# Attention products in 64-row and 64-column parts, two chunks in a bank for block 0, and an order by due times

## The chip, the cores and the metric

The kernel runs on one core of a Trainium2 chip. The metric is the device time of one execution in microseconds; before the change its median over three runs is 845.69 (844.81 to 847.82). In the text TensorE, VectorE, ScalarE, GpSimd and SyncE stand for the engines that the profile calls PE, DVE, ACT, POOL and SP.

## What is computed

A linear attention (4 batches, 8 heads, 576 tokens, 64 columns a head) gives 2304 tokens of 512 columns. Two feed-forward layers follow: a gated one of width 1536 behind a norm over the token, and an elu one of width 2048. All in fp32.

```
kv  = einsum('bhsd,bhse->bhde', k, v)
out = einsum('bhsd,bhde->bhse', q, kv)
x   = out / sqrt(mean(out * out, -1) + 1e-6) * g_norm      # per head
x   = (per token: heads side by side, 2304 x 512)
xn  = x / sqrt(mean(x * x, -1) + 1e-6) * rms_g
x   = (silu(xn @ w_gate) * (xn @ w_val)) @ w_out           # 512 -> 1536 -> 512
g   = elu(x @ w_in)                                        # 512 -> 2048
y   = g @ w_out2                                           # 2048 -> 512
```

## The kernel before

**Tiles.** The 2304 tokens are 18 tiles of 128 rows, two to a pair. Five blocks carry them through the layers: block 0 has one pair (256 columns), blocks 1 to 4 have two pairs each (512 columns), and blocks (1,2) and (3,4) also work together. A batch is 576 tokens, four and a half tiles, so tiles 4 and 13 lie across two batches. The hidden width is cut into chunks f of 128: 12 in the gated layer (phase 0), 16 in the elu layer (phase 1).

**Numbers in two parts.** Each operand of the large products is a high part (h_g, xh, act 0) and a low part (l_g, xl, act 1), and a product is three of them: high by high, low by high, high by low. A weight comes from memory as raw (raw_g) and is taken apart by `conversion` (line 401): c_g, w_g, then h_g on ScalarE and l_g on VectorE. For names in the list `SPARE` two of its steps run on ScalarE (lines 412 and 435) and not on VectorE (lines 414 and 437).

**Attention.** `sum_kv` (line 260) adds the k by v products of one tile into the bank of its batch: four products of two heads each, 128 by 128, of which only the two 64 by 64 blocks on the diagonal are wanted. `keep_kv` copies these blocks into a buffer whose other blocks were set to zero. `attend` (line 295) multiplies q of one tile with that buffer, four products of 128 by 128 into one bank po; a tile across two batches does it for each half of its tokens, with 64 columns of weights. On po follow the square on ScalarE (line 313), the mean on VectorE (317), the power on GpSimd (324), the product with it on VectorE (327), the product with g_norm (333), the same over the whole token (338 to 345), and `turn` (line 353), which transposes a pair into banks pt. From pt, line 371 makes xh (ScalarE) and line 369 xl (VectorE). An fp32 product is two matmul instructions in the trace.

**The layers.** hid_g and hid_v (line 754) are the products of the first weights for one f and one block, named hid_g(phase, f, block). The pair units pu and pb (lines 552 and 920) do two f, two blocks at a time. The way back b(group, block, chunk) (line 654) multiplies with w_out; for all but the last group its bank is copied by ScalarE (line 692) and added to `mid` in memory by a transfer of GpSimd's queue (line 698); the first group is written by SyncE. For the last group the sum so far is fetched (line 717) and added on VectorE (line 728, far), and xh and xl of the next layer come from that (lines 1305 and 1308), with sums T of blocks for the pair units (976 to 983).

**The order.** Nothing is written in the program's order by hand. Every piece of work is a step of `Plan` with an engine, a length, the steps it needs and the banks or buffers it takes. `run` (line 73) goes through time: on each engine it takes the ready step that can start first, and among those within 0.03 us the one with the lowest rank, a number written by hand (100 + 100 i for tile i's attention, higher for later f). The buffers are given out in the same pass. The order that results is the program of each engine.

## Time and profile before

| | us |
|---|---|
| median of three runs | 845.69 |
| profiled execution | 845.66 |
| span of the profiled execution | 843.9 |
| TensorE busy | 830.4 (98%) |
| VectorE busy | 742.2 (88%) |
| ScalarE busy | 593.0 (70%) |
| GpSimd busy | 228.5 (27%) |

Phase 0 begins within the attention at about 38 us, the pair units at about 100, and phase 1 at about 470. Busy time of TensorE is that of matmuls whose ends overlap, so a full stretch shows no idle time, and what a piece of work costs is read from start to start: a group of n alike instructions lasts n - 1 of these steps and one instruction's own time (0.27 us for a small fp32 matmul). A line of a stretch gives busy time, the granted clock as a share of 2.4 GHz, and how much of the 16 DMA engines' time was used.

### The profile page before, as it was taken

How to read it: one execution, taken by the hardware profiler on the slowest of the kernel's cores; microseconds unless marked ns; L12 is line 12 of the kernel's file. 1: busy time of each engine (PE TensorE's matmuls, PEld its weight loads, DVE VectorE, ACT ScalarE, POOL GpSimd, SP SyncE). 2: the span in 40 equal slices, each digit the busy share in tenths (PEclk: the TensorE clock that was granted, in tenths of full speed). 3: DMA queues.
4: the chain of work that ended last, by engine and by line, in shares of the span. 5: the costliest groups of instructions: out<-in, count | busy, mean ns of one | idle time of the engine just before them, and what ended most of it. 6: DMA issues, size and time to landing. Idle time of an engine off the chain costs nothing.

```text
span 843.9 us, 12231 instructions
## 1 busy us (share of the span) xinstructions
PE 830.4 (98%) x4108; PEld 695.2 (82%) x4108; DVE 742.2 (88%) x1375; ACT 593.0 (70%) x1149; POOL 228.5 (27%) x260
## 2 busy tenths in 40 slices
...
PEclk9999999999999999999999999999999999999999
...
GB/s 361 365 161 44 124 159 180 109 163 166 46 55 148 149 75 136 125 65 134 142 187 94 81 141 154 144 150 125 162 189 137 116 150 207 105 146 156 159 264 208
DMA packets 57375, 126.14 MB, mean 149 GB/s; under 512 B 6496, under 2 KB 10080, under 8 KB 57312
## 3 DMA queue, kind: packets, MB, share of 16 engines
...
HBM read 59.28 MB, written 66.06 MB: 149 GB/s over the span
## 4 chain that ended last, share of the span: by engine, by line
PE 82%; DVE 10%; DMA 3%; ACT 2%; issue 1%; SPq 0%; ACTq 0%; DVEq 0%
PE b L654 15%; PE hid_v L754 4%; PE hid_g L754 4%; PE po L304 2%; PE hid_i L754 2%; DMA wacc<-in_q 1%; DVE far L728 1%; PE kv L268 1%; DMA wacc<-in_kv 1%; DVE T L983 1%; DVE act L608 1%; DVE xl L1308 1%; DVE far L976 1%; PE pt L359 1%; PE ('pu', 1, 0, 3)_a L552 1%
## 5 line engine op out<-in xcount | busy, mean ns | idle before, releaser
L952 POOL DMA_DIRECT2D out<-part x80 | 70.3, 965 | 259.6 <-DVE part L939 211.0
L952 POOL DMA_DIRECT2D mid<-part x48 | 42.5, 970 | 149.0 <-DVE part L939 128.3
L654 PE MATMUL b<-act,h_o 128*128 128x512 f32 (+1 forms) x288 | 78.4, 358 | 1.3 <-DVE far L728 0.7
L698 POOL DMA_DIRECT2D mid<-part x52 | 46.6, 989 | 92.8 <-ACT part L692 89.3
L692 ACT ACTIVATE part<-b 128x512 f32<-128x512 f32 (+1 forms) x118 | 62.9, 552 | 9.8 <-PE b L654 5.0
L654 PEld LDWEIGHTS b<-act,h_o 128*128 128x128 f32 x288 | 51.0, 188 | 12.3 <-DVE far L728 1.8
L654 PE MATMUL b<-act,h_p 128*128 128x512 f32 x192 | 59.8, 392 | 1.4 <-ACT part L692 0.7
L654 PE MATMUL b<-act,l_o 128*128 128x512 f32 (+1 forms) x144 | 51.0, 354 | 0.0
L795 ACT ACTIVATE e<-e 128x512 f32<-128x512 f32 (+1 forms) x80 | 46.5, 590 | 0.7
L654 PEld LDWEIGHTS b<-act,h_p 128*128 128x128 f32 x192 | 35.7, 188 | 9.8 <-ACT part L692 1.3
L654 PE MATMUL b<-act,l_p 128*128 128x512 f32 x96 | 37.4, 389 | 0.0
L324 POOL TENSOR_TENSOR ri<-ms,nhalf 128x8 f32<-128x8 f32 x18 | 31.3, 1759 | 13.9 <-DVE ms L320 13.9
L754 PE MATMUL hid_g<-xh,h_g 128*128 128x256 f32 (+1 forms) x96 | 32.9, 343 | 0.0
L754 PE MATMUL hid_g<-xl,h_g 128*128 128x256 f32 (+1 forms) x96 | 32.5, 338 | 0.3 <-DVE xl L369 0.3
L698 POOL DMA_DIRECT2D out<-part x28 | 24.6, 895 | 30.0 <-ACT part L692 29.6
L754 PE MATMUL hid_v<-xh,h_v 128*128 128x256 f32 (+1 forms) x96 | 32.5, 339 | 0.0
L754 PE MATMUL hid_g<-xh,l_g 128*128 128x256 f32 (+1 forms) x96 | 32.3, 337 | 0.0
L754 PE MATMUL hid_v<-xh,l_v 128*128 128x256 f32 (+1 forms) x96 | 32.3, 336 | 0.0
L754 PE MATMUL hid_v<-xl,h_v 128*128 128x256 f32 (+1 forms) x96 | 32.3, 336 | 0.0
L728 DVE TENSOR_TENSOR far<-far,b 128x512 f32<-128x512 f32 (+1 forms) x38 | 24.2, 654 | 8.9 <-PE b L654 5.9
L654 PEld LDWEIGHTS b<-act,l_o 128*128 128x128 f32 x144 | 27.1, 188 | 3.8
L885 DVE TENSOR_TENSOR e<-e,e 128x512 f32<-128x512 f32 x40 | 27.3, 684 | 0.0
...
## 6 DMA issues: line engine op xcount, KB each, us to landing
out<-part POOLq DMA_DIRECT2D x108, 256.0 KB, 6.1
...
```

What stands on the lines that cost most here:

```text
L268: nc.tensor.matmul(kv_acc[b][:, p, :], in_sb[i][r0:r1, p * P:(p + 1) * P], in_sb[i][r0:r1, DM + p * P:DM + (p + 1) * P], start=(i == tiles ...
L304: nc.tensor.matmul(po[r:r1, p * P:(p + 1) * P], qt[:, p, r:r1], kv_sb[b][:, p, :], start=True, stop=True)
L324: nc.gpsimd.tensor_tensor(ri, ms_t.pop(i), nhalf, op=ALU.pow)
L359: nc.tensor.transpose(pt[:, c, k * P:(k + 1) * P], x, ident)
L654: nc.tensor.matmul(po, l, r, start=f == fs[0] and i == 0, stop=f == fs[-1] and i == 2)
L692: nc.scalar.activation(x, pbank["b", k, t, e][:, :n], AF.Copy)
L698: nc.gpsimd.dma_start(out=where(ph, t, e), in_=live.pop(key), accum_op=ALU.add)
L728: nc.vector.tensor_tensor(x, x, pbank["b", k, t, e][:, :n], op=ALU.add)
L754: nc.tensor.matmul(pbank[key], l, r, start=c == 0 and i == 0, stop=c == KD - 1 and i == 2)
L795: nc.scalar.activation(live[key], live[key], AF.Exp, scale=-1.0)
L885: nc.vector.tensor_tensor(raw(*into), raw(*x), raw(*y), op=ALU.subtract)
L952: lambda key=key, t=t, e=e: nc.gpsimd.dma_start(out=where(ph, t, e), in_=live.pop(key), accum_op=ALU.add),
```

## The change

**Attention's products.** kv is made of eight products of a tile, one for each head: 128 rows, 64 columns of weights, 64 moving columns. Even heads go to the left half of TensorE's columns, odd ones to the right. One ScalarE copy of 128 by 256 takes the place of two, and no buffer has to be zeroed. q's products go by pairs of tiles: each has 64 rows (one head), 128 tokens of weights, 64 moving columns. Even heads fill the bank po(pair, 0), odd ones po(pair, 1). Square, mean, power and the product with it then go by pair and side, with as many instructions of the same number of elements as before; the rest goes by tile as before. A whole pair is one step of the plan.

**Block 0's way back in phase 0.** Two chunks of 256 columns share a bank, so copies, transfers, sums and low parts come as two of 512 columns in place of four of 256.

**Conversions.** `SPARE` begins at f = 2, not 4: for g, v and o of f = 2 and 3, twelve steps go from VectorE to ScalarE. The last pair unit of phase 0 takes its buffers from the attention's.

**The order.** The old pass comes first. Then up to six times: going back from TensorE's order, each step gets the latest time at which it has to be done, with the buffers as they were given out; these times become the ranks, and a second kind of pass makes a new order with the buffers fixed. The order with the earliest planned end is used.

```diff
-    def run(self):
-        waits = {n: sum(1 for _ in s["after"]) for n, s in self.steps.items()}
-        then = {}
-        for n, s in self.steps.items():
-            for x in s["after"]:
-                assert x in self.steps, (n, x)
-                then.setdefault(x, []).append(n)
+    def order(self):
+        self.holder, self.where = dict(self.held), {}
+        self.ends, self.log, self.rooms = {}, [], []
+        self.clock = dict(self.start)
...
+                if slot in self.holder:
+                    self.rooms.append((self.holder[slot], n))
...
+    def again(self):
+        after = {n: list(s["after"]) for n, s in self.steps.items()}
+        for key, taker in self.rooms:
+            after[taker] += self.users[key]
...
+    def latest(self):
+        need = {n: list(self.then.get(n, ())) for n in self.steps}
+        for key, taker in self.rooms:
+            for u in self.users[key]:
+                need[u].append(taker)
+        late, t = {}, 0.0
+        for _, n, e, length in self.log:
+            if e == "PE":
+                late[n] = t
+                t += length
+        for _, n, e, length in reversed(self.log):
+            s = self.steps[n]
+            ends = [late[x] - self.LAG[e][self.steps[x]["engine"] != e] - s["lat"] for x in need[n] if x in late]
+            here = min(ends, default=t) - length
+            late.setdefault(n, here)
+        return late
+
+    PASSES = 6
...
+        end = self.order()
+        assert end, "no step can start"
+        best = end, self.log
+        for _ in range(self.PASSES):
+            late = self.latest()
+            for n, s in self.steps.items():
+                s["rank"] = late[n]
+            end = self.again()
+            if end < best[0]:
+                best = end, self.log
+        self.log = best[1]
...
-SPARE = [f"{x}{f}" for f in range(4, 12) for x in "gvo"] + [f"{x}{f}" for f in range(2, 16) for x in "ip"]
+SEEDS = ()
+SPARE = [f"{x}{f}" for f in range(2, 12) for x in "gvo"] + [f"{x}{f}" for f in range(2, 16) for x in "ip"]
...
-        "A": AD, "A1": ["y0", "t3"], "P": P3 + K2, "U": US, "C": CS,
+        "A": AD, "A1": ["y0", "t3"], "P": P3 + K2, "U": US, "UZ": Z4 + ["t2"], "C": CS,
...
+    zz = [res.tile([P, 2, DM + 1], F32, tag=f"zz{j}", name=f"zz{j}") for j in range(Z // 2)]
+    z_sb = [zz[j // 2][:, j % 2, :] for j in range(Z)]
...
-        for p in range(KD):
-
+        for h in range(H):
+            s = slice(h % 2 * D, (h % 2 + 1) * D)
             nc.tensor.matmul(
-                kv_acc[b][:, p, :],
-                in_sb[i][r0:r1, p * P:(p + 1) * P],
-                in_sb[i][r0:r1, DM + p * P:DM + (p + 1) * P],
-                start=(i == tiles[0] and p == 0),
+                kv_acc[b][s, h // 2 * D:(h // 2 + 1) * D],
+                in_sb[i][r0:r1, h * D:(h + 1) * D],
+                in_sb[i][r0:r1, DM + h * D:DM + (h + 1) * D],
+                start=(i == tiles[0] and h < 2),
...
-    def keep_kv(b, h):
-        t = kv_sb[b] = kv_blocks[b % 2]
-        s = slice(h * D, (h + 1) * D)
-        nc.scalar.activation(t[s, :, s], kv_acc[b][s, :, s], AF.Copy)
+    def keep_kv(b):
+        kv_sb[b] = kv_blocks[b % 2]
+        nc.scalar.activation(kv_sb[b], kv_acc[b], AF.Copy)
...
-    def attend(i):
-
-        qt = q_sb[i // 2].rearrange("d (j a t) -> d j a t", j=2, a=KD)[:, i % 2]
-        po = bank(("po", i))
-        r = 0
-        while r < P:
-            b = (i * P + r) // seq
-            r1 = min(P, (b + 1) * seq - i * P)
-            for p in range(KD):
-                nc.tensor.matmul(
-                    po[r:r1, p * P:(p + 1) * P], qt[:, p, r:r1], kv_sb[b][:, p, :], start=True, stop=True
-                )
-            r = r1
-        po_t[i] = po.rearrange("p (h d) -> p h d", h=H)
-
-
-    def square(i):
+    def side(p, s):
+        j = 2 * p % Z
+        return zz[j // 2][:, :, :DM].rearrange("p t (a s d) -> p t a s d", s=2, d=D)[:, :, :, s]
+
+    def attend(p):
+
+        qt = q_sb[p].rearrange("d (j a t) -> d j a t", j=2, a=KD)
+        po = [bank(("po", p, s)).rearrange("p (t a d) -> p t a d", t=2, d=D) for s in range(2)]
+        for j in range(2):
+            i = 2 * p + j
+            for a in range(KD):
+                r = 0
+                while r < P:
+                    b = (i * P + r) // seq
+                    r1 = min(P, (b + 1) * seq - i * P)
+                    for s in range(2):
+                        k = slice(s * D, (s + 1) * D)
+                        nc.tensor.matmul(
+                            po[s][r:r1, j, a, :], qt[k, j, a, r:r1], kv_sb[b][k, a * D:(a + 1) * D], start=True, stop=True
+                        )
+                    r = r1
+        for s in range(2):
+            po_t[p, s] = po[s]
+
+    def square(p, s):
...
+        nc.scalar.activation(side(p, s), po_t[p, s], AF.Square, scale=D**-0.5)
+
+    def mean(p, s):
+        ms = ms_t[p, s] = sp.tile([P, H], F32, tag="ms", name=f"ms{p}_{s}")
+        nc.vector.tensor_reduce(ms.rearrange("p (t a) -> p t a", t=2), side(p, s), axis=AX.X, op=ALU.add)
+
+    def guard(p, s):
+        nc.vector.tensor_scalar(ms_t[p, s], ms_t[p, s], EPS, None, op0=ALU.add)
+
+    def invert(p, s):
+        ri = ri_t[p, s] = sp.tile([P, H], F32, tag="ri", name=f"ri{p}_{s}")
+        nc.gpsimd.tensor_tensor(ri, ms_t.pop((p, s)), nhalf, op=ALU.pow)
+
+    def norm(p, s):
+        ri = ri_t.pop((p, s)).rearrange("p (t a) -> p t a", t=2).unsqueeze(3).to_broadcast([P, 2, KD, D])
+        nc.vector.tensor_tensor(side(p, s), po_t.pop((p, s)), ri, op=ALU.mult)
...
+    KV, PO = 0.6, 1.1
...
+        if ph == 0 and t == 0:
+            for j in range(2):
+                s = slice((2 * e + j) * P, (2 * e + j + 1) * P)
+                for i, (l, r) in enumerate(((wh, ah), (wh, al), (wl, ah))):
+                    nc.tensor.matmul(
+                        po[:, j * n:(j + 1) * n], l[:, s], r, start=first and i == j == 0, stop=f == fs[-1] and i == 2,
+                        skip_group_check=True,
+                    )
+            return
...
-            return mid[:, e, a * P:(a + m) * P]
+            return mid[:, e, a * P:(a + m) * P] if t else mid[:, 2 * e:2 * e + 2, a * P:(a + m) * P]
...
-                    nc.gpsimd.dma_start(out=where(ph, t, e), in_=live.pop(key), accum_op=ALU.add)
+                    nc.gpsimd.dma_start(out=where(ph, t, e), in_=flat(live.pop(key), t or ph), accum_op=ALU.add)
...
-                nc.sync.dma_start(out=x, in_=where(ph, t, e))
+                nc.sync.dma_start(out=flat(x, t or ph), in_=where(ph, t, e))
...
+        if i % 2 == 0:
+            bs = sorted({(i * P) // seq, (i * P + 2 * P - 1) // seq})
+            old = [("turn", p - Z // 2, half) for half in range(2)] if i >= Z else []
+            plan.add(
+                ("po", p), "PE", PO, r, lambda p=p: attend(p), [("in", f"q{p}"), *[("kept", b) for b in bs], *old],
+                [("o0", ("po", p, s)) for s in range(2)],
+            )
...
+        for e in range(KD if X else 2):
...
+                nc.vector.tensor_tensor(flat_x(xl), fetched[0, t, e], flat_x(xh).bitcast(F32), op=ALU.subtract)
+
+            n = W
```

How this moves instructions, at three places.

TensorE, where the attention starts. kv_0 is the bank of batch 0; wxh2, wxl2, wacc0 hold tiles of k and v, wxl3 holds q; the number behind a name is that of the buffer. Before:

```order
L268 MATMUL kv_0_117<-wxh2_113 128x128 x8
L268 MATMUL kv_0_117<-wxl2_127 128x128 x8
L268 MATMUL kv_0_117<-wacc0_151 128x128 x4
L268 MATMUL kv_1_168<-wacc0_151 128x128 x4
L304 MATMUL po_0_183<-kv0_107,wxl3_160 128x128 x4
L304 MATMUL po_1_193<-kv0_107,wxl3_160 128x128 x4
L268 MATMUL kv_1_168<-wacc1_188 128x128 x8
L268 MATMUL kv_1_168<-wacc2_210 128x128 x8
```

After:

```order
L353 MATMUL kv_0_112<-wxh2_108 64x64 x16
L353 MATMUL kv_0_112<-wxl2_126 64x64 x16
L353 MATMUL kv_0_112<-wacc0_158 64x64 x8
L353 MATMUL kv_1_183<-wacc0_158 64x64 x8
L396 MATMUL po_0_0_199<-kv0_104,wxl3_171 128x64
L396 MATMUL po_0_1_200<-kv0_104,wxl3_171 128x64
```

A row now stands for 64 by 64 products (a tile has 8), and q's products alternate between the two banks of a pair.

TensorE, where block 1 enters phase 0 (xh1, xl1 are its tokens). Before, ahead of hid_g_0_0_1:

```order
L754 MATMUL hid_g_0_1_0_517<-xh0_338,h_g1_480 128x256
L754 MATMUL hid_g_0_1_0_517<-xl0_339,h_g1_480 128x256
L754 MATMUL hid_g_0_1_0_517<-xh0_338,l_g1_495 128x256
L654 MATMUL b_0_0_0_538<-act_0_0_0_0_488,h_o0_224 128x256 x2
L654 MATMUL b_0_0_0_538<-act_0_0_0_0_488,l_o0_231 128x256
L654 MATMUL b_0_0_1_545<-act_0_0_0_0_488,h_o0_224 128x256 x2
L654 MATMUL b_0_0_1_545<-act_0_0_0_0_488,l_o0_231 128x256
L754 MATMUL hid_g_0_0_1_552<-xh1_497,h_g0_143 128x512
L754 MATMUL hid_g_0_0_1_552<-xl1_498,h_g0_143 128x512
L754 MATMUL hid_g_0_0_1_552<-xh1_497,l_g0_148 128x512
```

After:

```order
L396 MATMUL po_4_0_627<-kv0_104,q_4_561 128x64
L396 MATMUL po_4_1_628<-kv0_104,q_4_561 128x64
L450 MATMUL pt_2_0_650<-ident_88,zz2_69 128x128 x4
L450 MATMUL pt_2_1_658<-ident_88,zz2_69 128x128 x4
L875 MATMUL hid_g_0_0_1_675<-xh1_597,h_g0_150 128x512
L875 MATMUL hid_g_0_0_1_675<-xl1_598,h_g0_150 128x512
L875 MATMUL hid_g_0_0_1_675<-xh1_597,l_g0_155 128x512
```

The products of chunk 1 for block 0 (hid_g_0_1_0) and the way back of block 0 stood there; now the transposes of pair 2 stand there, behind the q products of pair 4, while b_0_0 was earlier and hid_g_0_1_0 comes later.

VectorE, ahead of the last low halves of block 1 (xl1 from pt_2). Before:

```order
L774 TENSOR_TENSOR sa_0_0_445<-sa_0_0_445,hid_v_0_0_0_439 128x256
L327 TENSOR_TENSOR z0_67<-po_6_385,ri6_451 128x512
L449 SCALAR_TENSOR_TENSOR l_g1_495<-w_g1_458,h_g1_480 128x512
L608 TENSOR_TENSOR act_0_0_0_0_488<-sa_0_0_445,act_0_0_0_0_488 128x256
L333 TENSOR_TENSOR z0_67<-z0_67,gains_sb_98 128x512
L369 SCALAR_TENSOR_TENSOR xl1_498<-pt_1_0_483,gains_sb_98,xh1_497 128x256 x2
L369 SCALAR_TENSOR_TENSOR xl1_498<-pt_1_1_490,gains_sb_98,xh1_497 128x256 x2
L369 SCALAR_TENSOR_TENSOR xl1_498<-pt_2_0_502,gains_sb_98,xh1_497 128x256 x2
L369 SCALAR_TENSOR_TENSOR xl1_498<-pt_2_1_510,gains_sb_98,xh1_497 128x256 x2
```

After:

```order
L520 SCALAR_TENSOR_TENSOR w_g1_600<-raw_g1_487,c_g1_572 128x512
L419 TENSOR_TENSOR zz0_67<-po_3_0_489,ri3_0_574 128x2x4x64
L460 SCALAR_TENSOR_TENSOR xl1_598<-pt_1_0_565,gains_sb_95,xh1_597 128x256 x2
L460 SCALAR_TENSOR_TENSOR xl1_598<-pt_1_1_592,gains_sb_95,xh1_597 128x256 x2
L529 TENSOR_SCALAR c_g1_572<-raw_g1_487 128x512
L532 ISA w_g1_600<-w_g1_600,c_g1_572 128x1024
L506 TENSOR_SCALAR c_v1_664<-raw_v1_589 128x512
L419 TENSOR_TENSOR zz0_67<-po_3_1_490,ri3_1_625 128x2x4x64
L460 SCALAR_TENSOR_TENSOR xl1_598<-pt_2_0_650,gains_sb_95,xh1_597 128x256 x2
L460 SCALAR_TENSOR_TENSOR xl1_598<-pt_2_1_658,gains_sb_95,xh1_597 128x256 x2
```

The product of tile 6 with gains_sb and l_g1 no longer stand ahead of xl1; the first step of v1's conversion and the second norm of pair 3 do.

## Rows read from the trace of the kernel before

**Rows 1.** The page: span, busy us (share) of an engine, and 40 slices in tenths.

```profile
span 843.9 us, 12231 instructions
PE 830.4 (98%) x4108; PEld 695.2 (82%) x4108; DVE 742.2 (88%) x1375; ACT 593.0 (70%) x1149; POOL 228.5 (27%) x260
...
PEclk9999999999999999999999999999999999999999
```

**Rows 2.** Stretches: length, busy us (instructions) of engines, granted clock, DMA share, GB/s.

```profile
0.00:40.00 40.00, 35.52 (x280) 33.68 (x281) 27.77 (x58) 19.55 (x42) 16.85 (x29) 1.00 0.97 380
...
102.00:165.00 63.00, 62.10 (x285) 50.77 (x286) 63.00 (x122) 38.10 (x72) 15.85 (x17) 1.00 0.72 149
460.00:500.00 40.00, 37.41 (x174) 29.83 (x173) 38.79 (x72) 28.86 (x53) 0.00 (x0) 1.00 0.32 102
628.00:633.00 5.00, 4.31 (x18) 2.76 (x17) 5.00 (x10) 5.00 (x13) 0.87 (x1) 1.00 0.44 130
822.00:828.00 6.00, 5.29 (x30) 4.31 (x29) 5.18 (x10) 5.94 (x14) 0.00 (x0) 1.00 0.88 266
838.00:843.90 5.90, 2.08 (x10) 1.39 (x8) 1.46 (x3) 0.00 (x0) 0.00 (x0) 0.91 0.40 152
```

**Rows 3.** Waits of TensorE: line, releaser, us in total, times, longest.

```profile
PE kv L268 <- DMA wacc<-in_kv: 1.3, 1, 1.3
PE ('pu', 1, 0, 3)_a L552 <- DVE ('pu', 1, 0, 1)_u L578: 1.2, 1, 1.2
...
PE po L304 <- POOL gains_sb L376: 0.9, 1, 0.9
...
PE hid_g L754 <- DVE xl L369: 0.3, 1, 0.3
```

**Rows 4.** Instructions of lines 268 and 304: ns min/median/max, first and last start, forms.

```profile
L268 PE MATMUL kv<-wacc x64: 272/275/377, 12.7 to 36.9; 128*128 128x128 f32 x48, 64*128 64x128 f32 x16
...
L304 PEld LDWEIGHTS po<-kv,wacc x40: 132/192/192, 22.9 to 28.1; 128*128 128x128 f32 x24, 128*64 128x64 f32 x16
```

**Rows 5.** Timeline of TensorE, narrow windows: start, us, rows*columns of the part used.

```profile
22.89 3.56 PE L304 MATMUL po<-kv,wacc 128*128 128x128 f32 x32
...
28.27 1.95 PE L268 MATMUL kv<-wxh 128*128 128x128 f32 x16
...
24.67 1.78 PE L304 MATMUL po<-kv,wacc 128*128 128x128 f32 x17
...
25.03 0.98 PE L304 MATMUL po<-kv,wacc 128*64 128x128 f32 x11
...
12.99 0.94 PE L268 MATMUL kv<-wacc 64*128 64x128 f32 x10
...
30.94 0.61 PE L268 MATMUL kv<-wxl 128*128 128x128 f32 x4
...
31.48 0.49 PE L268 MATMUL kv<-wxh 64*128 64x128 f32 x2
```

**Rows 6.** Timeline around 46 us and at 205 us; idle before in brackets.

```profile
44.23 3.22 DVE L369 SCALAR_TENSOR_TENSOR xl<-pt,gains_sb,xh 128x256 fp32r<-128x256 f32 x8
...
46.03 0.47 PE L654 MATMUL b<-act,h_o 128*128 128x256 f32 x2 [0.19 <-DVE xl L369]
...
46.46 0.40 PE L754 MATMUL hid_g<-xh,h_g 128*128 128x512 f32 x1
...
205.07 0.39 PE L552 MATMUL ('pu', 0, 4, 1)_a<-xh,h_g 128*128 128x512 f32 x1
```

**Rows 7.** Waits of VectorE in the first 36 us.

```profile
DVE c_g L414 <- DMA raw_g<-in_w_gate: 4.7, 1, 4.7
DVE ms L317 <- ACT z L313: 2.3, 3, 1.2
```

**Rows 8.** Groups by line: busy us, mean ns, idle before (VectorE to 48 us; ScalarE).

```profile
L437 DVE TENSOR_SCALAR c_g<-raw_g 128x512 uint32<-128x512 uint32 x2 | 0.9, 426 | 0.1
...
L435 ACT ACTIVATE c_g<-raw_g 128x512 uint32<-128x512 uint32 x8 | 5.4, 669 | 5.8 <-DVE w_g L428 5.8
```

188 lines of the change are left out of this document (113 added, 75 removed).

## Prediction

> **What bounds the kernel now.** I read the busy shares first, then a table of stretches, then who waits for whom, then single instructions. TensorE is busy for 830.4 of the 843.9 us of the span, VectorE for 742.2, and the granted clock is 9 tenths or more (full speed, 2.4 GHz) in every slice [rows 1]. So time goes only where TensorE gets less work, or where one of its few gaps closes. The stretches show where the gaps are: 4.48 us in the first 40, 2.59 between 460 and 500, 0.90 between 102 and 165, 0.69 and 0.71 around 630 and 825, and 3.8 in the tail [rows 2]. DMA is at 0.97 of its engines in the first 40 us, and VectorE is busy for 63.00 of the 63 us from 102 to 165 and for 38.79 of 40 from 460 to 500 [rows 2]. The waits name the releasers: k/v tiles that are still on their way (1.3 us), the gains (0.9), the last low halves of block 1's tokens, and at 488 a sum on VectorE (1.2) [rows 3].
>
> The attention that the change cuts into lies before 100 us, and most of it where TensorE waits already. That is the question: does the freed time reach the dense part? The profiled execution took 845.66 us, the median of the runs is 845.69, so the sum can be put on the median as it stands.
>
> **kv products.** All of the 160 kv instructions of TensorE run before 42 us; the largest of three alike groups has 64 of 275 ns each [rows 4]. Pipelined, 16 of them follow each other in (1.95 - 0.27) / 15 = 0.112 us [rows 5], so one token tile with its 8 costs 0.89 us. After, a tile has 16 instructions, each with 64 columns of weights and 64 moving columns, in two column halves. A load of 64 columns lasts 133 ns where one of 128 lasts 192 [rows 4], which is 59 ns less, so 0.111 - 0.059, some 0.055 us from start to start in one half. If the halves run side by side, a tile costs 8 x 0.055 = 0.44 to 0.46 us. That they do is seen once: 11 matmuls of column halves start within 0.98 - 0.27 us, 0.071 us apart, and ten of row halves 0.074 apart, where whole ones stand 0.106 apart (32 in 3.56 us) [rows 5]. 20 tile parts x 0.43 = **8.6 us less work for TensorE**, all ahead of 42 us. The bounds: 20 x 0.89 = 17.8 us less is out of reach; nothing less, if the halves run in turn. One rule speaks against this edit: by the Trainium skill, "TensorE: Matmul & The Clock Gate", section "Part 3: Packing small matmuls — row/col tiling", a weight load overlaps matmuls in flight only where its row group is another one. Both column halves use all rows, so by that rule no load here would be hidden and the time would be that of the fourth rival; the starts 0.071 us apart do not agree with it.
>
> **Products with q.** A pair of token tiles had 16 fp32 products of 128 columns, 32 instructions, 3.56 us for two pairs [rows 5], so 1.78 a pair. After, it has 16 products of 64 rows; the moving columns are halved, but the weights are still 128 columns of q, so I keep 0.111 us from start to start in one row half: 16 instructions in each half, side by side, 1.78 us again. Only in pairs 2 and 6, where one tile lies across two batches, that tile comes in 64 by 64 parts, with loads of 64 columns: 0.45 us for it, 1.34 for the pair. The changed plan counts 1.1 us for a pair; I don't follow it, since the weight load is what the row shows to set the pace. Its end (0.055 us apart, 0.9 us a pair) goes into the first rival.
>
> **What reaches the dense part.** The first product of block 1, hid_g(0,0,1), starts at 46.46, and the back product ahead of it waited for xl [rows 6], the eight low halves that VectorE makes from 44.23 to 47.4 [rows 6]. In the changed order the rows of VectorE up to the last of these are the same work less 0.3 us: a multiplication by the gains and l_g1 (0.68 us each) fall behind, a step of v1's conversion (0.42) and a norm (0.68) come ahead. VectorE was busy 27.77 us in the first 40 [rows 2]; of its 12.2 idle us 4.7 wait for the first weight and 2.3 for squares on ScalarE [rows 7]. The first stays, since the loads of k, v, q and the first weights are issued in the same order and DMA is full. Of the second I take 0.7 us, since faster kv work makes only some squares earlier. So hid_g(0,0,1) comes 1.0 us earlier (0 to 3), and **some 7 of the 8.6 us become waiting** ahead of it. Who is late next there is VectorE, not TensorE.
>
> Behind hid_g(0,0,1) TensorE's own work counts. Before, ten tiles of q products lay there, nine of 0.89 us and tile 13, divided like tile 4, whose 16 instructions stood (1.78 - 0.27) / 16 = 0.094 us apart [rows 5], at 1.5: 9.5 us. After, pairs 5 to 8: 3 x 1.78 + 1.34 = 6.7. That is 2.8 us less. The order takes hid_g(0,1,0), 12 products at 0.12 us, behind it (+1.44) and two chunks of block 0's way back ahead of it (-0.72): +0.7. A change of the form of the matmuls costs time: the last of four whole kv instructions starts at 30.94 + 0.61 - 0.27 = 31.28, the next, of another form, at 31.48 [rows 5], 0.20 instead of 0.11. The changed order has nine such changes there instead of two: 7 x 0.093 = +0.65. Net 1.45 us, with the 1.0 above **2.45 us**.
>
> **Conversions of f = 2 and 3.** Twelve more instructions go from VectorE (0.42 us) to ScalarE (0.67) [rows 8]: VectorE has 5.0 us less in the stretch from 102 to 165 where it never rests, ScalarE 8.0 more, at 38.10 busy of 63 [rows 2]. ScalarE hides that. I take the 0.90 us that TensorE lacked there as gained. Bounds: nothing, if the conversions themselves come later through ScalarE; more than 0.90, since a matmul that starts late but touches its forerunner's modelled end shows no gap.
>
> **Block 0's way back with two chunks in a bank.** TensorE's products are the same (256 columns each). ScalarE's copies out of the bank become 12 of 512 columns in place of 24 of 256, POOL issues 10 fewer accumulations and SP 4 fewer transfers, none of which waited on the path. Cost nothing, hidden by ScalarE's 70% [rows 1]; cover gone, a copy of 0.55 us would hold a bank longer. VectorE's sums and low halves at 460 to 500 shrink from four instructions of 0.41 us to two of 0.68, twice: 0.56 us. It is the engine that TensorE waits for there [rows 2, 3], so 0.5 us is gained.
>
> **Order by due times.** It can't take work away. The two small gaps at 630 and 825 hold 1.4 us [rows 2]; I take 0.5, with bounds of 1.4 gained and 2.6 (the size of the largest gap once more) lost. Sum: 2.45 + 0.90 + 0.5 + 0.5 = 4.35; 845.7 - 4.35 = **841.4 us** (rounded), 839 to 843 with the nearer bounds.
>
> **Rivals.** (1) *The front gives way as well.* The due times fill VectorE's waits, up to the 6 us that aren't waits for weights, hid_g(0,0,1) comes 3 us earlier still, and the pairs run nearer to 1.1 us. For it: VectorE's rows ahead of it do hold work that could be put off. Against it: those loads are at the limit of the DMA. 841.4 - 3 - 4 x (1.78 - 1.1) = 835.7.
>
> (2) *VectorE takes it back at the change of phase.* From 460 to 500 it has 1.2 us of rest. By a count of its rows, with the durations of before, the changed order has some 2.7 us more of VectorE's work ahead of the product that waited 1.2 us there. If that isn't hidden, 841.4 + 2.7 = 844.1, and with no gain between 102 and 165, 845: no change that can be told. The same time comes if the front gives nothing and the order nothing.
>
> (3) *Slower: the row halves run in turn.* Then a pair costs 3.56 us. Five pairs lie ahead of hid_g(0,0,1), and 8.9 us more there fill the 7 us of waiting and 1.9 beyond; four lie behind it, and they cost 4 x 1.78 = 7.1: 841.4 + 1.9 + 7.1 = 850. It decides from about 1 us a pair on, when the gain is gone. Against it are the starts 0.074 us apart in row halves [rows 5]; for it, that those came in blocks of four products and the new ones alternate, each into another bank, with full weight loads.
>
> (4) *Slower: in column halves no load overlaps a matmul in flight.* A kv tile part then costs 16 x 0.11 = 1.8 us, 20 x 1.3 = 26 us more, of which 7 are covered: 860. The starts 0.071 us apart in column halves [rows 5] speak plainly against it. It is the mechanism of the page's rule above.
>
> **How the numbers follow.** The forecast has 0.43, rival (1) 0.20, rival (2) with its no change 0.20, (3) 0.13 and (4) with what I haven't thought of 0.04. This kernel's runs tell about 0.3% (2.5 us) from no change, so faster means under 843.2 and slower over 848.2. Faster: 0.43 + 0.20 less a little of the forecast's upper end, 0.61; same: 0.20 + 0.01; slower: 0.18, which takes in 0.01 of rival (2). The range leaves out the best tenth and rival (4) with the worse half of (3): 834.5 to 849.5.
>
> **What would show it.** In the trace after: kv tiles of 16 instructions in some 0.45 us; q pairs in 1.78 (0.9 would be rival 1, 3.6 rival 3); hid_g(0,0,1) at 45 to 46 with more idle TensorE ahead of it; pu(0,4,1)_a, at 205.07 before [rows 6], at 201 to 203; a gap near 484 of 2 to 3 us. I am wrong if hid_g(0,0,1) starts before 43 or if the gaps from 460 to 500 exceed 5 us.

## The result, and the profile after

The change makes the kernel slower, by less than one per cent: 854.07 us (847.69 to 855.61, seven runs) against 845.32 (844.81 to 847.82) for the kernel before, a ratio of 1.0085 with a 95% interval of 1.0067 to 1.0102. The profiled execution is one of the shorter ones, 849.73 us with a span of 848.0. The accounts below are made on it, against 845.66 and 843.9 before; what lies between it and the median comes at the end of this part.

The page after: span, busy us of an engine (share), 40 slices in tenths.

```profile
span 848.0 us, 12808 instructions
...
PE 832.2 (98%) x4428; PEld 695.4 (82%) x4428; DVE 740.9 (87%) x1359; ACT 595.7 (70%) x1143; POOL 218.8 (26%) x248
...
PEclk7799999999999999999999999999999999999999
```

Against [rows 1], TensorE is no less busy (832.2 for 830.4), though its attention work was to shrink by over 8 us. The line PEclk says why: the first two slices are no longer at full clock. Stretches after (columns as in [rows 2]):

```profile
5.00:10.00 5.00, 4.08 (x64) 3.48 (x62) 3.10 (x6) 0.63 (x1) 0.00 (x0) 1.00 1.00 375
10.00:15.00 5.00, 2.66 (x52) 2.35 (x52) 3.61 (x7) 0.81 (x2) 0.19 (x1) 0.74 1.03 409
15.00:20.00 5.00, 5.00 (x62) 4.79 (x62) 1.86 (x4) 1.29 (x3) 0.00 (x0) 0.50 1.03 410
...
30.00:35.00 5.00, 5.00 (x76) 4.25 (x73) 2.69 (x6) 2.93 (x7) 2.30 (x3) 0.71 1.02 407
...
460.00:500.00 40.00, 36.88 (x168) 29.36 (x166) 37.56 (x65) 27.16 (x48) 0.00 (x0) 0.96 0.36 110
```

From about 12.4 to 32.9 us the granted clock is 0.50, which is 1.2 GHz. Ahead of the drop TensorE was busy for 4.08 and 2.66 of two stretches of 5 us, since it waited for k and v. The same two stretches before the change:

```profile
5.00:10.00 5.00, 4.94 (x37) 4.75 (x36) 3.10 (x6) 0.63 (x1) 0.00 (x0) 1.00 0.98 388
10.00:15.00 5.00, 3.38 (x29) 2.81 (x27) 3.75 (x8) 1.06 (x3) 0.19 (x1) 1.00 1.02 408
```

The timeline of TensorE after, in the narrow windows that answer to [rows 5 and 6] (start, us, instructions of one kind in a row, idle before in brackets):

```profile
7.09 1.46 PE L353 MATMUL kv<-wxh 128*64 128x64 f32 x32
9.18 0.69 PE L353 MATMUL kv<-wxl 128*64 128x64 f32 x16 [0.64 <-DMA wxl<-in_kv]
11.75 0.69 PE L353 MATMUL kv<-wxl 128*64 128x64 f32 x16 [1.88 <-DMA wxl<-in_kv]
13.02 1.61 PE L353 MATMUL kv<-wacc 64*64 64x64 f32 x32 [0.59 <-DMA wacc<-in_kv]
14.63 3.68 PE L396 MATMUL po<-kv,wxl 64*128 64x64 f32 x32
18.23 2.15 PE L353 MATMUL kv<-wacc 128*64 128x64 f32 x32
20.54 1.12 PE L353 MATMUL kv<-wacc 128*64 128x64 f32 x16 [0.16 <-DMA wacc<-in_kv]
...
47.44 1.97 PE L396 MATMUL po<-kv,q 64*128 64x64 f32 x30 [1.04 <-DVE xl L460]
49.34 1.09 PE L450 MATMUL pt<-ident,zz 128*128 128x128 f32 x8
50.56 0.49 PE L875 MATMUL hid_g<-xh,h_g 128*128 128x512 f32 x1
51.45 0.50 PE L875 MATMUL hid_g<-xl,h_g 128*128 128x512 f32 x1 [0.39 <-DVE xl L460]
...
479.67 0.93 PE L644 MATMUL ('pu', 1, 0, 1)_a<-T,Sh_i 128*128 128x512 f32 x2 [2.45 <-ACT ('pu', 1, 0, 1)_u L667]
```

The instructions do nearly what was forecast. At full clock the 16 kv instructions of a tile take 0.69 us with the last one's own 0.22, so 0.47 / 15 = 0.031 us from start to start and 0.50 a tile. Of a pair of q 30 of the 32 instructions go from 47.44 to 49.34, which makes 2.0 us for all, and at half clock a pair takes 3.60 (14.63 to 18.23).

But hid_g(0,0,1) starts at 50.56, where it stood at 46.46 [rows 6]: 4.1 us later, not 1.0 earlier. The other marks: pu(0,4,1)_a at 208.86 (205.07 before), pu(1,0,3)_a at 493.72 (487.90), the end of the span at 847.96 (843.86). So the whole profiled difference reads as

- up to hid_g(0,0,1): +4.1 us,
- from there to pu(0,4,1)_a: 158.30 in place of 158.61, -0.3,
- to pu(1,0,3)_a: 284.86 in place of 282.83, +2.0, among it the wait of 2.45 at 479.67 for a copy of ScalarE,
- to the end: 354.24 in place of 355.96, -1.7.

The engine that TensorE waits for last around hid_g(0,0,1) is VectorE, as before: 1.04 us for low halves ahead of the q products at 47.44, and 0.39 us for hid_g's own second product. Waits of VectorE in the first 50 us after (line, releaser, us in total, times, longest), and its busy time there:

```profile
DVE ms L408 <- ACT zz L404: 6.2, 5, 3.0
DVE c_g L506 <- DMA raw_g<-in_w_gate: 4.8, 1, 4.8
...
0.00:50.00 50.00, 44.19 (x586) 40.02 (x587) 33.10 (x69) 21.71 (x47) 17.99 (x28) 0.80 0.82 317
```

VectorE does 33.10 us of work in 50 us; before it did 33.71 in 46 us:

```profile
0.00:46.00 46.00, 41.27 (x327) 39.05 (x327) 33.71 (x70) 23.93 (x53) 19.49 (x30) 1.00 0.88 344
```

Its idle time ahead of hid_g(0,0,1) went from 12.3 to 16.9 us, by 4.6, and 3.9 of that is the wait for squares on ScalarE, 2.3 in [rows 7] and 6.2 now. Whether the half clock or the products by pairs make the squares late, this trace alone can't say. Nor does it tell what the longer runs hold. Of the changed kernel's seven runs those with a mean granted clock of 0.981 or 0.982 took 854.1 to 855.6 us, the one with 0.988 took 847.7; but two with 0.984 took 853.7 and 854.5, and in a_again below 0.984 goes with 849.8 and 850.8.

### The profile page after: what moved, and what is told of

It reads as the page before. It is cut to its first block, busy times and chain, and to the rows that moved or that the text cites. A ratio compares the mean times of both kernels' runs of the same rounds, so it can differ in the third digit from the quotient of the medians.

```text
span 848.0 us, 12808 instructions
## 1 busy us (share of the span) xinstructions
PE 832.2 (98%) x4428; PEld 695.4 (82%) x4428; DVE 740.9 (87%) x1359; ACT 595.7 (70%) x1143; POOL 218.8 (26%) x248
## 4 chain that ended last, share of the span: by engine, by line
PE 76%; DVE 13%; DMA 5%; ACT 4%; issue 2%; SPq 0%; DVEq 0%; ACTq 0%
PE b L755 12%; PE hid_g L875 4%; PE hid_v L875 3%; PE hid_i L875 2%; PE po L396 2%; PE b L743 1%; DMA wacc<-in_q 1%; DVE far L849 1%; DMA wacc<-in_kv 1%; DMA raw_g<-in_w_gate 1%; DMA mid<-part 1%; ACT part L810 1%; DVE act L701 1%; DVE xl L1430 1%; DVE far L1097 1%
## 5 line engine op out<-in xcount | busy, mean ns | idle before, releaser
L1073 POOL DMA_DIRECT2D mid<-part x48 | 42.5, 957 | 161.2 <-DVE part L1060 79.4
L810 ACT ACTIVATE part<-b 128x512 f32<-128x512 f32 x106 | 61.8, 594 | 11.6 <-PE b L755 7.4
L816 POOL DMA_DIRECT2D mid<-part x42 | 40.8, 1008 | 86.8 <-ACT part L810 86.0
L755 PE MATMUL b<-act,h_o 128*128 128x512 f32 x192 | 60.1, 394 | 0.0
L755 PEld LDWEIGHTS b<-act,h_o 128*128 128x128 f32 x192 | 36.0, 190 | 8.0 <-issue 0.6
L755 PE MATMUL b<-act,l_o 128*128 128x512 f32 x96 | 37.6, 392 | 0.0
L816 POOL DMA_DIRECT2D out<-part x28 | 24.3, 878 | 34.3 <-ACT part L810 31.9
L849 DVE TENSOR_TENSOR far<-far,b 128x512 f32<-128x512 f32 x36 | 24.1, 683 | 8.0 <-PE b L755 5.9
L697 ACT ACTIVATE act<-zz 128x512 fp32r<-128x512 f32 (+1 forms) x37 | 20.9, 565 | 14.2 <-DVE zz L895 5.2
L916 ACT ACTIVATE zz<-zz 128x512 f32<-128x512 f32 (+1 forms) x41 | 24.0, 596 | 0.2
L701 DVE TENSOR_TENSOR act<-zz,act 128x512 fp32r<-128x512 f32 (+1 forms) x37 | 22.4, 607 | 0.9 <-ACT act L697 0.8
```

The source lines that it names most:

```text
L697: nc.scalar.activation(acts[ph, f, t][0], src(), AF.Copy)
L701: nc.vector.tensor_tensor(l, src(), h.bitcast(F32), op=ALU.subtract)
L755: nc.tensor.matmul(po, l, r, start=first and i == 0, stop=f == fs[-1] and i == 2, skip_group_check=seeded(ph, k, t))
L810: nc.scalar.activation(x, pbank["b", k, t, e][:, :n], AF.Copy)
L816: nc.gpsimd.dma_start(out=where(ph, t, e), in_=flat(live.pop(key), t or ph), accum_op=ALU.add)
L849: nc.vector.tensor_tensor(x, x, pbank["b", k, t, e][:, :n], op=ALU.add)
```

## The experiments

The times of all kernels, each against runs of the kernel before on the same chip. The marks are starts in the profiled execution: hid_g(0,0,1), pu(0,4,1)_a, pu(1,0,3)_a, and the end of the span.

| kernel | median us | ratio, 95% interval | hid_g | pu(0,4,1) | pu(1,0,3) | end |
|---|---|---|---|---|---|---|
| before | 845.32 | | 46.46 | 205.07 | 487.90 | 843.86 |
| changed | 854.07 | 1.0085 (1.0067 to 1.0102) | 50.56 | 208.86 | 493.72 | 847.96 |
| a_again | 850.72 | 1.0064 (1.0048 to 1.0081) | 50.57 | 209.07 | 493.68 | 848.04 |
| a_filled | 849.00 | 1.0043 (1.0027 to 1.0059) | 50.62 | 208.86 | 493.01 | 847.27 |
| a_kvwhole | 848.27 | 1.0033 (1.0015 to 1.0051) | 52.77 | 210.58 | 493.81 | 848.13 |
| a_fill_early | 851.69 | 1.0068 (1.0045 to 1.0091) | 50.03 | 211.44 | 496.58 | 850.91 |
| a_handorder | 859.85 | 1.0167 (1.0152 to 1.0182) | 52.27 | 216.91 | 502.58 | 858.08 |
| b_kv | 845.03 | 0.9989 (0.9979 to 0.9998) | 45.72 | 204.53 | 487.44 | 843.38 |
| b_order | 841.81 | 0.9959 (0.9943 to 0.9975) | 46.69 | 204.22 | 485.04 | 839.14 |
| b_order_kv | 842.29 | 0.9957 (0.9942 to 0.9972) | 47.08 | 204.67 | 486.06 | 839.74 |
| b_plan06 | 849.76 | 1.0046 (1.0031 to 1.0061) | 46.95 | 203.26 | 487.74 | 848.32 |
| m_att | 865.74 | 1.0246 (1.0230 to 1.0261) | 54.31 | 219.53 | 503.81 | 863.58 |
| m_att_fill | 860.86 | 1.0179 (1.0157 to 1.0200) | 48.62 | 214.67 | 498.91 | 859.29 |
| m_att_order | 851.78 | 1.0075 (1.0058 to 1.0092) | 51.08 | 212.26 | 497.42 | 850.07 |
| m_att_order_po19 | 849.21 | 1.0044 (1.0030 to 1.0058) | 52.03 | 209.42 | 494.68 | 846.70 |
| m_nochunk_po19 | 849.15 | 1.0042 (1.0030 to 1.0054) | 50.60 | 208.59 | 492.26 | 847.60 |
| m_spare | 851.70 | 1.0067 (1.0044 to 1.0090) | 46.05 | 204.94 | 489.53 | 849.95 |
| m_block0 | 846.62 | 1.0013 (1.0004 to 1.0023) | 46.36 | 204.28 | 490.60 | 844.69 |
| m_spare_order | 844.56 | 0.9986 (0.9975 to 0.9997) | 47.38 | 205.65 | 491.35 | 843.52 |
| m_noatt | 851.57 | 1.0071 (1.0051 to 1.0091) | 47.41 | 204.26 | 486.92 | 847.42 |

Names with a_ start from the changed kernel, with b_ from the one before; m_ are single parts of the change put into the kernel before. The changed kernel itself, run in two series (changed and a_again), has medians 3.4 us apart, where the kernel before lay between 845.32 and 845.68 in all of its series.

### Is it the clock?

**a_filled**: the changed kernel with two products more behind each kv tile, into a part of the bank that nobody reads. TensorE's lost work comes back, as filler.

```
+        for _ in range(2):
+            nc.tensor.matmul(kv_bank[b][:, HALF:HALF + P], in_sb[i][:, :P], in_sb[i][:, DM:DM + P], ...)
```

> The changed kernel, and behind the products of each kv tile two fp32 products of 128 by 128 whose result nobody reads, so that a tile costs TensorE 0.9 us as in the kernel before; nothing else moves. Theory clock: the trace of the changed kernel shows a granted clock of 0.5 from 12.7 to 32.5 us, after TensorE stood idle for 3.4 of the 6 us from 7 to 13; with that time filled the clock stays at 1.0, hid_g(0,0,1) starts at 45 to 47 and the time is 841 to 845.5. Rival order: the new order makes TensorE wait for VectorE ahead of hid_g(0,0,1) in any case; the clock comes back and the time stays above 848. Rival cost: the filler simply adds its 9 us, 852 and more.

Measured 849.0, with a clock of 0.998 to 1.0 in its four runs. The two stretches ahead of the former drop, and VectorE's waits:

```profile
5.00:10.00 5.00, 4.94 (x73) 4.31 (x71) 3.55 (x8) 0.63 (x1) 0.00 (x0) 1.00 1.02 412
10.00:15.00 5.00, 4.84 (x72) 4.05 (x72) 3.73 (x7) 0.90 (x2) 0.19 (x1) 1.00 1.03 402
...
DVE ms L414 <- ACT zz L410: 4.7, 5, 1.4
DVE sa L901 <- PE hid_v L881: 2.7, 1, 2.7
```

With TensorE busy like this the clock does not fall in the front, and no run is over 849.4 us, though four runs say little: a_again's four, at half clock, have none over 852.2. The time fits the rival "order", above 848. hid_g(0,0,1) starts at 50.62, as late as at half clock, but that alone does not clear the clock, for the filler stands on the path: TensorE is busy for 18.89 of the 19.00 us from 31.60 to 50.60, seven fillers lie there, some 3.7 us by an estimate from their starts, and VectorE waits 2.7 us for hid_v. What the kernel does show is that VectorE waits 4.7 us for squares at full clock, where it waited 2.3 before; the other 1.5 of the changed kernel's 6.2 are gone with the half clock.

**a_kvwhole**: the kv products whole again, all else changed.

```
-        for h in range(H):
+        for p in range(KD):
-                kv_acc[b][s, h // 2 * D:(h // 2 + 1) * D],
+                kv_acc[b][:, p, :],
```

> The changed kernel with the kv products as before (four of 128 by 128 a tile, two copies out of the bank), the order as planned with the short products, so the sequence on each engine is the changed one. Theory clock: like the filled kernel within 1 us, clock 1.0, 841 to 845.5. Rival order: above 848 at a clock of 1.0.

848.27 us, hid_g(0,0,1) at 52.77, and half clock still, from 22.5 to 32.7 us, which neither expectation had. The column halves alone are not what makes hid_g late.

**a_fill_early** makes the kv products of the first nine tiles twice (the second time into the unread part), and **m_att_fill** does that to m_att below.

```
+        again = 1 if b == 0 or (b == 1 and i > tiles[0]) else 0
+        for n, h in [(n, h) for n in range(1 + again) for h in range(H)]:
```

> The changed kernel with the kv products of the first two batches (tiles 0 to 8, which wait for their loads) made twice, the second time into the unused half of the same bank, which nobody reads: TensorE's idle time ahead of 22 us gets filled, and unlike in the filled kernel no work is added behind that. Theory clock: the clock stays at 1.0 and hid_g(0,0,1) comes at 45 to 47 in place of 50.6, so the time is 843 to 846. Rival VectorE: pairs of tiles hold VectorE's chain back whatever the clock; hid_g(0,0,1) stays at 49 or later and the time at 847 to 849.

> Attention's products in parts alone, by hand ranks (865.7 so far, with TensorE at half clock from 12 to 21, 32 to 42 and 54 to 59 us), with the same early kv products made twice. Theory clock: the first drop goes; if it takes the later ones with it, 850 to 858. Rival VectorE: 862 and more.

In a_fill_early the half clock does not go, it comes later: at 31.9 to 35.3 and 48.9 to 52.4 us. hid_g(0,0,1) starts at 50.03: with 4.5 us of half clock ahead of it in place of some 20, it is only 0.5 us earlier. The time, 851.69 us, lies above both expectations. In m_att_fill, up to 165 us, the half clock is gone, where m_att had it for nearly 24 us:

```profile
0.00:50.00 50.00, 40.94 (x549) 36.48 (x549) 28.14 (x59) 19.20 (x44) 16.86 (x26) 0.80 0.81 314
...
0.00:50.00 50.00, 41.62 (x733) 36.76 (x733) 33.84 (x71) 24.78 (x57) 19.76 (x30) 1.00 0.85 327
```

The first line is m_att's, the second m_att_fill's. hid_g(0,0,1) comes 5.7 us earlier there (48.62 for 54.31) and the median falls by 4.9 us, between the two expectations. So in the order by hand the half clock does cost time in the front, and at full clock attention's parts still delay hid_g by 2.2 us (48.62 for 46.46). How much of the changed kernel's 4.1 us is the clock's these runs do not settle: a_filled has filler on the path, and a_fill_early has half clock left on it.

**a_again**: the changed kernel once more.

> The changed kernel as it is, once more, for another profile, since its times lie between 847.7 and 855.6 and the profiled execution took 849.73. Theory (the spread is TensorE's granted clock in the front): an execution of 853 us or more shows over 22 us at half clock, and hid_g of the first block starts later than 50.56 us by most of the difference. Rival (the spread arises elsewhere): the half-clock stretch ends near 32.5 us and hid_g starts near 50.6 us whatever the total.

850.72 us at 0.984 to 0.986. It has a second drop, where the first profile had none:

```profile
45.00:50.00 5.00, 3.96 (x55) 3.59 (x54) 4.82 (x10) 3.27 (x7) 3.23 (x4) 0.94 0.30 105
50.00:55.00 5.00, 4.91 (x19) 3.65 (x18) 4.09 (x9) 4.51 (x12) 0.64 (x2) 0.72 0.60 213
```

Yet hid_g(0,0,1) starts at 50.57 and the span ends at 848.04, within 0.1 us of the first profile. The second drop, from 49.4 to 52.8 us, begins barely ahead of hid_g, and the first is as long as in the first profile. So 3.4 us more of half clock cost nothing at the end that these two profiles show; what the first 20 us cost they can't tell. The four runs are 1.7 us above a_filled, the first seven 5.1. The executions of 853 us and more were never caught with a profile, and what they hold stays open.

### Which part?

**b_kv** (kv in column halves alone), **b_order** (order by due times alone) and **b_order_kv** (both).

```
+                kv_acc[b][s, h // 2, s],
+                in_sb[i][r0:r1, h * D:(h + 1) * D],
+                in_sb[i][r0:r1, DM + h * D:DM + (h + 1) * D],
```

```
+        for _ in range(self.PASSES):
+            late = self.latest()
+            for n, s in self.steps.items():
+                s["rank"] = late[n]
+            end = self.again()
```

> The kernel before with one part of the change alone: the kv products as eight 64-column products of a tile in two column halves; order, copies and all else as before. Theory clock: TensorE has 8.6 us less work in the first 42 us, mostly as idle time between loads, so the granted clock falls to 0.5 for 10 to 30 us, and the time is 847 to 855. Rival order: the clock stays, the time is 845 or a little less.

> The kernel before with the order by due times alone (same products, same conversions). Theory clock: the work of TensorE in the front is whole, the clock stays at 1.0, 843 to 846. Rival order: the waits for VectorE and ScalarE of the changed kernel's front come from the order, 848 to 852 at a clock of 1.0.

> The order by due times with the kv products in column halves, q's products by tiles. Theory clock: a short drop as with kv in halves alone (0.5 from 14 to 21 us, which cost nothing there since k/v tiles were awaited anyway), 840 to 843. Rival: the order leaves no slack in the front, the drop costs its length, 844 to 848.

The column halves are harmless and bring next to nothing: hid_g(0,0,1) comes 0.7 us earlier, and the rest of the freed time becomes waiting. b_kv too runs at half clock for a while, from 13.4 to 20.2 us, with TensorE busy for 1.91 of the 5 us from 10 to 15, at no cost (a drop as one theory had it, though a shorter one, and the time of its rival):

```profile
10.00:15.00 5.00, 1.91 (x48) 1.58 (x48) 3.90 (x8) 1.30 (x3) 0.19 (x1) 0.84 1.03 410
15.00:20.00 5.00, 4.82 (x38) 4.63 (x40) 4.49 (x10) 1.60 (x4) 0.85 (x1) 0.50 1.02 409
```

The order alone is the best kernel of all, 3.8 us below the kernel before on its chip (845.64) and below both expectations, with b_order_kv beside it. Its gain lies far behind the attention: 0.85 us at pu(0,4,1), 2.9 at pu(1,0,3), 4.7 at the end. In the stretch from 460 to 500 TensorE is busy for 1.14 us more than in [rows 2], and from 500 to 640, where it lacked 0.69 before, it has no gap at all:

```profile
460.00:500.00 40.00, 38.55 (x179) 30.92 (x179) 38.56 (x72) 28.77 (x55) 0.00 (x0) 1.00 0.33 103
500.00:640.00 140.00, 140.00 (x647) 115.79 (x646) 129.15 (x237) 120.70 (x235) 34.22 (x40) 1.00 0.73 151
```

**m_att** (all of the attention's edits, old order), **m_att_order** (the same with due times) and **a_handorder** (the whole change with the old order).

```
-    PASSES = 6
+    PASSES = 0
```

> The kernel before with attention's products in parts alone, in the order by hand ranks. Theory attention by itself: a pair's products, squares and powers hold VectorE's chain back in any order, 848 to 854. Rival: only the order by due times, which counts 1.1 us for a pair that takes 1.9, makes it costly; then 843 to 847 here.

> The order by due times with attention's products in parts (kv halves, q by pairs) and the buffers of the last unit, without the conversions and without two chunks in a bank. Theory attention: 847 to 855, with hid_g(0,0,1) at 49 or later, as in the changed kernel. Rival conversions and banks: 840 to 844.

> The whole change in the order by hand ranks, without the passes by due times. If the order gives the changed kernel what it gives the kernel before (3.9 us): 852 to 860. If the order is what makes the parts of attention costly: 843 to 848.

m_att lies above both expectations, the other two in the ranges of the first theory. The order is not what makes attention's parts costly: with it, and other buffers for one late unit, m_att falls by 14.0 us, and a_handorder is 5.8 us above the changed kernel's 854.07, or 9.1 above a_again.

m_att_order and b_order_kv differ in q's products and the norm by pairs, and in little else (the plan's lengths for them, the single copy of kv, the buffers of one late unit). That costs 9.5 us, 851.78 against 842.29, and 4.0 of it stand at hid_g(0,0,1) (51.08 against 47.08). Each has an order of its own, whose worth is unknown (see b_plan06), and m_att_order has half clock for 20.5 us where b_order_kv has it for 6.8. What carries the finding is the table: in all eleven kernels with pairs hid_g(0,0,1) starts between 48.62 and 54.31, in all nine without them between 45.72 and 47.41. The waits of VectorE in m_att_order:

```profile
DVE ms L407 <- ACT zz L403: 7.2, 5, 3.0
```

and in b_order_kv:

```profile
DVE ms L400 <- ACT z L396: 3.4, 5, 1.0
```

Why they are late can be read at pairs 0 to 2 in a_filled, at full clock. VectorE there and, from 24.66 on, ScalarE:

```profile
21.58 0.69 DVE L425 TENSOR_TENSOR zz<-po,ri 128x512 f32<-128x512 f32 x1
...
23.20 0.69 DVE L425 TENSOR_TENSOR zz<-po,ri 128x512 f32<-128x512 f32 x1 [0.16 <-POOL ri L421]
23.93 1.29 DVE L430 TENSOR_TENSOR zz<-zz,gains_sb 128x512 f32<-128x512 f32 x2
...
29.65 0.69 DVE L414 TENSOR_REDUCE ms<-zz 128x8 f32<-128x512 f32 x1 [1.44 <-ACT zz L410]
...
33.68 0.68 DVE L430 TENSOR_TENSOR zz<-zz,gains_sb 128x512 f32<-128x512 f32 x1
...
24.66 0.64 ACT L435 ACTIVATE junk<-zz 128x513 bf16<-128x513 f32 x1 [1.71 <-DVE zz L430]
...
25.29 0.58 ACT L410 ACTIVATE zz<-po 128x512 f32<-128x512 f32 x1
...
28.40 1.22 ACT L410 ACTIVATE zz<-po 128x512 f32<-128x512 f32 x2
```

and in the kernel before:

```profile
20.76 0.69 DVE L327 TENSOR_TENSOR z<-po,ri 128x512 f32<-128x512 f32 x1 [0.17 <-POOL ri L324]
21.48 0.69 DVE L333 TENSOR_TENSOR z<-z,gains_sb 128x512 f32<-128x512 f32 x1
...
25.05 0.69 DVE L317 TENSOR_REDUCE ms<-z 128x8 f32<-128x512 f32 x1 [1.25 <-ACT z L313]
...
29.17 0.69 DVE L333 TENSOR_TENSOR z<-z,gains_sb 128x512 f32<-128x512 f32 x1
...
24.42 0.60 ACT L313 ACTIVATE z<-po 128x512 f32<-128x512 f32 x1
```

Before, each tile had its own norm (z from po and ri), and the product with the gains came right behind it, at 21.48 for the first tile. By pairs and sides, a tile is whole only when both sides have their norm, so that product comes at 23.93, 2.45 us later, with the first norm itself 0.82 late (21.58 for 20.76). ScalarE waits 1.71 us for it with the square over the token (junk), and the squares of pair 1 stand behind that in ScalarE's order: the first starts at 25.29 for 24.42. The first product with the gains of pair 1 starts at 33.68, where it stood at 29.17. TensorE was in time, since the products of pair 1 begin at 22.48 here, and its 32 instructions are through by 24.5; before they began at 22.89 [rows 5].

The pairs bring a second wait. In the plan a mean needs only its own square, and before it starts right behind it: 24.42 + 0.60 = 25.02, the mean at 25.05. With pairs the two sides lie in one buffer zz, in turns of 64 columns, and the mean of the first side starts behind the square of the second: two squares from 28.40 to 29.62, the mean at 29.65, though its own square was done at 28.99. In all eleven kernels with pairs no mean of a first side runs during the square of the second; before, at four of nine pairs of tiles, the mean of one runs during the square of the next. In a_filled this holds VectorE for some 2.3 us at pairs 0, 2 and 3, about as much as its wait for squares has grown there (2.3 to 4.7). No run had the sides in buffers of their own, so that the shared buffer is the reason isn't shown.

Waits are not all of it, either. Between the products with the gains of pair 0 and those of pair 1 VectorE idles for 2.6 us in a_filled and for 2.3 before, but it also does 2.7 us more of work there, such as the second side's norm and low halves that the order puts ahead. Over the whole kernel each engine has about as much to do as before. That the pairs delay hid_g(0,0,1) is shown; how the delay divides between the unit of a pair, the shared buffer, the order and the half clock is not.

**m_spare** (conversions of f = 2 and 3), **m_block0** (two chunks in a bank), **m_spare_order** (the first with due times), **m_noatt** (both with due times).

```
-SPARE = [f"{x}{f}" for f in range(4, 12) for x in "gvo"] + ...
+SPARE = [f"{x}{f}" for f in range(2, 12) for x in "gvo"] + ...
```

```
+            return mid[:, e, a * P:(a + m) * P] if t else mid[:, 2 * e:2 * e + 2, a * P:(a + m) * P]
```

> The kernel before with the conversions of f = 2 and 3 on ScalarE alone, hand ranks. If the conversions cost time by themselves (order and conversions gave 844.6, the order alone 841.8): 847 to 850. If they are free or a gain, as forecast: 844 to 846.

> The kernel before with block 0's way back as two chunks in a bank alone, hand ranks. If the chunks cost the 7 us between order with conversions (844.6) and the same with chunks (851.6): 849 to 853. If that difference is one of the orders that came out, not of the chunks: 844 to 847.

> Order by due times and conversions of f = 2 and 3 on ScalarE (and the other buffers for the last unit), without attention's parts and without two chunks in a bank. The order alone gave 841.8, with conversions and chunks 851.6. If the chunks of block 0 are what costs it at the change of phase and at the end: 839 to 843 here. If the conversions are: 846 to 852.

> The kernel before with all of the change but attention's products and copies (and but the buffers of the last phase 0 unit): order by due times, conversions of f = 2 and 3 on ScalarE, two chunks in a bank for block 0. After the first four runs: the order alone gives 841.8, and with the clock kept whole the changed kernel stays at 849. Theory attention: the loss lies in the products by pairs of tiles, so this kernel is as good as the order alone, 839 to 843. Rival conversions and banks: one of these two parts costs the 6 us, 846 to 850.

m_block0 came out in its second range, m_spare just above its first one; m_spare_order lies between its two, and m_noatt above both. Up to pu(0,4,1) m_spare and m_block0 are small gains, 0.1 and 0.8 us, and m_noatt's is 0.8. Then they lose, m_spare far from where its conversions stand, m_block0 at the change of phase, where its own sums and low halves are: m_spare is 1.6 us late at pu(1,0,3) and 6.1 at the end, m_block0 2.7 and 0.8, and m_noatt, still 1.0 ahead at pu(1,0,3), 3.6 at the end. m_spare_order is 3.5 late at pu(1,0,3) and ends where the kernel before does. The conversions' own stretch and the one at the change of phase in m_spare:

```profile
102.00:165.00 63.00, 61.30 (x285) 50.65 (x285) 61.27 (x114) 45.69 (x85) 15.31 (x17) 1.00 0.74 155
460.00:500.00 40.00, 35.89 (x160) 27.14 (x159) 39.00 (x72) 28.37 (x52) 0.00 (x0) 0.96 0.32 100
```

VectorE has 1.7 us of rest now between 102 and 165, and TensorE is idle for 1.7, more than the 0.90 of [rows 2]. The wait of 2.45 us for a copy of ScalarE at the change of phase is no mark of the chunks alone: all eight kernels with chunks have it, at 1.6 us or more, but m_spare_order, m_att_order and both of the next part, without chunks, have it too, at 2.3 us. Whether the chunks cost m_block0 its 2.7 us there stays open.

### Is it the plan?

**m_att_order_po19**: the plan counts 1.9 us for a pair of q in place of 1.1. **m_nochunk_po19**: the changed kernel without block 0's part, with 1.9 for a pair and 0.5 for a kv tile.

```
-    KV, PO = 0.6, 1.1
+    KV, PO = 0.6, 1.9
```

> The order by due times with attention's parts (851.8), with one number of the plan changed: it counts 1.9 us for a pair of q tiles, as the traces show, in place of 1.1; the products are the same. Theory planning: with the right length the order no longer makes engines wait for pairs that aren't there yet, 843 to 848, VectorE's wait for squares ahead of 66 us falls from 6 us to 4 or less. Theory grain: a pair's squares come late because a bank holds half the heads of both tiles, whatever the plan; the wait stays at 5 us or more and the time at 849 to 854.

> The same with the conversions of f = 2 and 3 on ScalarE and 0.5 us for a kv tile in the plan: the whole change but two chunks in a bank, with lengths as measured. Theory planning: 840 to 846. Theory grain: hid_g(0,0,1) at 49 or later, 848 to 853.

m_att_order_po19 is 2.6 us better than m_att_order, but in both kernels hid_g(0,0,1) stays late (52.03, 50.60) and VectorE's wait for squares stays at 5 us and more, as the theory "grain" had it. The wrong length is not what delays the front.

**b_plan06**: the kernel before, with one number of the plan changed and every instruction the same.

```
-                ("kv", b, i), "PE", 0.9, ...
+                ("kv", b, i), "PE", 0.6, ...
```

> The kernel before, with nothing changed but one number of the order's planning: a kv tile counts 0.6 us for TensorE in place of 0.9. Every instruction and every tile is the same; only the order on the engines comes out otherwise. Theory (a new order alone moves the time by several microseconds, most of it far behind the edit): block (0, 4, 1) of gate and up starts within 1 us of 205.07, and the total lies at least 1.5 us off 845.3, anywhere between 840 and 852, with the difference arising behind 430 us. Rival (orders that this planner makes are worth the same, and the parts' losses behind 430 us come of the parts themselves): 844.5 to 846.

849.76 us: 4.2 us slower by a new order alone. It is 1.8 us ahead at pu(0,4,1) (the theory had within 1 us), level at pu(1,0,3), and 4.5 behind at the end. Stretches, and two waits of TensorE, one between 455 and 510 and one between 640 and 850:

```profile
460.00:500.00 40.00, 35.88 (x158) 27.17 (x158) 39.03 (x72) 29.05 (x54) 0.00 (x0) 0.96 0.32 102
640.00:820.00 180.00, 177.98 (x809) 145.47 (x808) 165.39 (x296) 144.89 (x279) 61.89 (x70) 1.00 0.84 148
...
PE b L654 <- ACT part L692: 2.2, 1, 2.2
...
PE ('pu', 1, 8, 3)_a L552 <- ACT ('pu', 1, 8, 3)_u L574: 1.1, 1, 1.1
```

The two stretches read like m_spare's, whose TensorE is busy for 35.89 and 177.96 us there. So two orders of the same instructions, this one and b_order's, lie at 849.8 and 841.8 us, and what m_spare, m_block0 and m_noatt lose behind 460 us can be their orders' doing. That it is isn't shown: the orders were not exchanged between kernels.

## Why the prediction was wrong

The forecast was 841.4 us (834.5 to 849.5), faster; the result is slower, and outside. Point by point:

- **kv products**: right. 0.50 us a tile for 0.44 to 0.46, column halves side by side. By the Trainium skill, "TensorE: Matmul & The Clock Gate", "Part 3: Packing small matmuls — row/col tiling", no load would have been hidden here; 32 instructions of column halves in 1.46 us don't agree with it. Rivals (3) and (4) fell, and with them the way I had thought the kernel could become slower.
- **q pairs**: 2.0 us for the forecast 1.78 and 0.09 for the change of form, nearly right.
- **The step that failed is VectorE's waiting for squares** ahead of hid_g(0,0,1): "Of the second I take 0.7 us", off 2.3. It grew to 6.2, and to 4.7 in a_filled at full clock, and VectorE's whole idle time up to hid_g from 12.3 to 16.9. I had counted VectorE's rows ahead of the last low half, found the same work, and let its waits shrink with faster products. I didn't ask what a unit of a pair does to the steps between the engines: the norm has its count of instructions unchanged, but the first of them that the next engine needs comes 2.45 us later, and the mean of one side comes behind the square of the other. The front's term is +4.1 in place of -1.0. Neither of my two signs of being wrong appeared: I had looked for hid_g too early, not too late.
- **The clock was nowhere in the forecast.** I wrote that 7 of 8.6 us become waiting, and did not ask what a TensorE that waits is granted. [rows 1] show full speed only for the busier TensorE of before. Between m_att and m_att_fill it is worth 5.7 us at hid_g(0,0,1). In the changed kernel its share of the 4.1 us, and of the 5.1 us between the medians of the changed kernel and a_filled, stays open: a_fill_early moved hid_g by 0.5 us only, with some half clock left.
- **Behind hid_g(0,0,1)** I had 1.45 us of TensorE's work and 0.90 of conversions; 0.3 came. Alone, the conversions gave 0.1 up to 205 us. The lower bound, nothing, is nearest to what these runs show. The further loss of 2.0 us at the change of phase has about the size of rival (2), 2.7 us, and a gap of 2.45 us came where I had named one of 2 to 3; but it is a wait for a copy of ScalarE, not for VectorE.
- **Block 0's way back**: 0.5 forecast; alone 0.8 gained at 205 us, 0.8 lost at the end. The 0.56 us less of VectorE between 460 and 500 does not show in its busy time, 38.80 in m_block0 and 38.79 before.
- **Order by due times**: 0.5 forecast, bounds of 1.4 gained and 2.6 lost; alone it gains 3.8 in the median and 4.7 in the profile. I had bounded it by the small gaps of the phase that I listed, but it also took 1.1 of the gap at the change of phase and the waits of the tail. In the changed kernel that gain is not there: pu(1,0,3) loses 2.0 behind pu(0,4,1), where b_order gains 2.0.
- **The sum itself**: the terms were added as if each left the rest as it was. Every part of the change makes the planner write a new order for 840 us of work, and b_plan06 and b_order show what that alone is worth, 4 us either way. A range that held this would have reached above 849.5.
